# Second-layer weights of a routed MLP laid in SBUF by eight neighbouring rows for each partition

## The chip, the cores and the metric

The kernel runs on one core of one Trainium2 chip. The metric is the device time of one execution in microseconds (us), over several runs. Inputs lie in the chip's memory (DRAM) at the start, and the output must lie there at the end. The core's engines run side by side: TensorE multiplies matrices, VectorE, ScalarE and GpSimd do the element-wise work, and SyncE issues transfers. SBUF is the on-chip memory of 128 partitions; PSUM is the smaller one that TensorE writes its products to.

## The reference, cut to what matters

Two stages follow each other. The first is an attention of polynomial features, whose result becomes 4352 rows of 128 numbers. The second sends each row to two of eight experts, and each expert is a two-layer network:

```python
def _moe_ref(x, w_gate, w_noise, noise, w1, w2):      # x: 4352 x 128
    N, D = x.shape
    E = w_gate.shape[1]                                # 8 experts
    logits = x @ w_gate
    noise_scale = np.log1p(np.exp(x @ w_noise))
    noisy_logits = logits + noise_scale * noise
    top2 = np.argpartition(-noisy_logits, 2, axis=1)[:, :2]
    ...                                                # top2_w: softmax over the two
    for e in range(E):
        for k in range(2):
            mask = top2[:, k] == e
            h = np.maximum(x[mask] @ w1[e], 0.0)       # w1[e]: 128 x 1024
            out[mask] += top2_w[mask, k, None] * (h @ w2[e])   # w2[e]: 1024 x 128
```

Everything is float32. What matters here is the pair `h = max(x @ w1, 0)` and `h @ w2`: the second product sums over the 1024 hidden units, and a sum does not care in which order its terms come, as long as row f of `w2` meets hidden unit f.

## The kernel before, in words

**Layout of the weights.** Both weight tensors are kept in SBUF for the whole run. `w1s` has the 128 inputs of a row on the partitions and the 1024 hidden units of each expert beside each other. `w2s` is `[128 partitions, 8 experts, FJ = 8 pieces, D = 128]`; piece j of partition p holds row 128*j + p of the expert's `w2`. Function `load_w(e)` (line 377) issues the two transfers of an expert on SyncE's queue, through the helper `dma` (the transfer itself is recorded at line 338). `load_w` is called for expert 0, then 1, then 2 to 5, and last 6 and 7; between these calls stand the loads of the next keys, values and queries and of the padding of the row store `xs`.

**Blocks and waves.** After the router the rows of each expert are scattered by GpSimd into a store in DRAM, `xs`, at increasing places for each expert. Function `block` (line 1030) takes one stretch of one expert's rows. A wave is eight blocks, one for each expert, with the same stretch. There are six waves: two of 128 rows, three of 256 rows, and a last one of 128 rows. With 128 rows a block has n = 1 row tile, with 256 it has n = 2. So three waves have n = 1 and three have n = 2.

**Inside a block.** The block's rows stand transposed in `bT` (128 inputs by 128 or 256 rows). Then, in groups of js = 4/n pieces of 128 hidden units:
- `first` (line 1092; the product is line 1094) does js products into a PSUM tile `hp`. The stationary operand, loaded into the array, is a slice of 128 columns of `w1s`; the moving operand is `bT`, 128*n columns.
- `relu` (line 1098) takes `hp` to the SBUF tile `h`, mostly on ScalarE (line 1102).
- `second` (line 1105; the product is line 1109) does 4 products into the PSUM tile `acc`. The stationary operand is a slice of 128 columns of `h`, the moving operand a piece of `w2s` (128 columns).

With n = 1 a block has 2 groups of 4 first and 4 second products. With n = 2 it has 4 groups of 2 first products, which move 256 columns each, and 4 second ones. At the end `acc` is copied to `y`, and GpSimd scatters `y` to the tensor `pairs` in DRAM (`pool_scatter`, line 805).

**What sets the order.** All work is recorded as jobs with an engine, an estimated cost and a priority; class `Plan` (line 38) puts the jobs in one order by these estimates (its `order`, line 88), and each engine's instructions stand in that order. The costs are functions of tile sizes (`mm`, `vec`, `act`). GpSimd's scatters are tied by an extra dependency to the latest eviction recorded before them (`paces`).

**Other lines that the profile and the prediction name.** Line 606: the features of keys and queries. 669: the sums of features times values. 717: transposes of features on TensorE. 728: the numerators, with 98 moving columns. 747: a VectorE sum over the four heads of `lh`, read with the heads innermost. 975: a VectorE sum over the eight experts of `f2`, read in order. 809: GpSimd's scatters. 1417: products without use at the beginning, which keep TensorE busy. 322: copies by ScalarE or VectorE. A function `outside` (line 1258) runs only if an expert gets more rows than planned; it loads its weights by itself and the change does not touch it.

Of the kernel before, what the change touches and what calls it, by code (L numbers as in the profile page):

```python
# [37 lines left out]
class Plan:  # L38
# [17 lines left out]
    def new(self, tag):  # L56
        return Buf(tag)
# [117 lines left out]
def kernel(  # L175
# [15 lines left out]
    P = nc.NUM_PARTITIONS  # L191
# [5 lines left out]
    FJ = F // P  # L197
# [30 lines left out]
    V, A, G, T, Y = nc.vector, nc.scalar, nc.gpsimd, nc.tensor, nc.sync  # L228
# [4 lines left out]
    def add(engines, cost, emit, **kw):  # L233

        if hold and engines in ("DVE", "PE"):
            kw["after"] = tuple(kw.get("after", ())) + tuple(hold)
        elif hold and engines == EV:
            engines = "ACT"
        return plan.add(engines, cost, emit, **kw)
# [65 lines left out]
    def mm(n):  # L305
        return max(0.205, 0.016 + 0.00162 * n)
# [6 lines left out]
    def either(n):  # L313
        return {"ACT": act(n), "DVE": vec(n)}
# [17 lines left out]
    def dma(q, o, i, r, w, prio, size=0, issue=0.45, after=(), done=None, margin=0.0):  # L332

        eng = {"SP": Y, "ACT": A, "POOL": G}
        waits = hold_dma[0]

        def emit(e):
            ins = eng[e].dma_start(o(), i())  # L338
            if waits is not None:
                behind(ins, "rows %d" % waits)  # L340
            if done:
                done(ins)
        job = add(q, issue, emit, r=r, w=w, prio=prio, lat=LAND, after=after, size=size)
        if waits is not None:
            held.setdefault(waits, []).append(job)
        job.margin = margin
        return job
# [26 lines left out]
    w1s = const.tile([P, E, F], F32, name="w1s")  # L374
    w2s = const.tile([P, E, FJ, D], F32, name="w2s")

    def load_w(e, prio):
        dma("SP", lambda: w1s[:, e, :], lambda: moe_w1[e], (), [("w1", e)], prio, size=524e3, issue=0.5)
        dma("SP", lambda: w2s[:, e, :, :], lambda: moe_w2[e].rearrange("(j p) d -> p j d", p=P),
            (), [("w2", e)], prio, size=524e3, issue=0.5)  # L380

    words = const.tile([2 * R, 2 * DH], U32, name="words")
# [400 lines left out]
    def behind(ins, *keys):  # L783
        for key in keys:
            for name in writers.get(key, ()):
                tc.add_manual_dep(ins.ins, name, DATA, reason="rows written before")
# [243 lines left out]
    def block(u, w, e, r, n):  # L1030
# [57 lines left out]
        js = 4 // n  # L1088
        for g in range(FJ // js):
            hp, h = new("hp"), new("h")  # L1090

            def first(_, g=g, hp=hp):
                for i in range(js):
                    T.matmul(hp.t[:, P * n * i:P * n * (i + 1)], lhsT=w1s[:, e, P * (js * g + i):P * (js * g + i + 1)],  # L1094
                             rhs=bT.t[:, 0:P * n], start=True, stop=True)
            add("PE", js * mm(P * n), first, lat=0.15, r=[bT, ("w1", e)], w=[hp], prio=p0 + 10 * g)

            def relu(en, hp=hp, h=h):
                if en == "DVE":
                    paces.append(V.tensor_scalar_max(h.t[:], hp.t[:], 0.0))  # L1100
                else:
                    paces.append(A.activation(out=h.t[:], in_=hp.t[:], func=AF.Relu))  # L1102
            add(EV, either(512), relu, r=[hp], w=[h], prio=TOP + u)

            def second(_, g=g, h=h):
                for i in range(js):
                    for c in range(n):
                        j = js * g + i
                        T.matmul(acc.t[:, D * c:D * c + D], lhsT=h.t[:, P * (n * i + c):P * (n * i + c + 1)],  # L1109
                                 rhs=w2s[:, e, j, :], start=(j == 0 and c == 0), stop=(j == FJ - 1), skip_group_check=True)  # L1110
            add("PE", 4 * mm(D), second, lat=0.15, r=[h, ("w2", e)], w=[acc], prio=p0 + 10 * g + 15)
# [238 lines left out]
    rest_of_queries = keys_values(0, 0, head=True)  # L1350
    load_kq(1, "k", 40)
    load_w(0, 41)
    first_loads = len(plan.jobs)
    for r in (0, P):
        clear(r, 43)
    load_w(1, 44)
    for e in range(2, E - 2):
        load_w(e, 46 + e)
# [98 lines left out]
```

## Time and profile before

| | |
|---|---|
| median of 3 runs | 353.58 us (353.15 to 354.06) |
| the profiled execution, as timed | 354.19 us |
| its span, from the first to the last instruction | 352.4 us |
| mean granted clock of TensorE | 0.996 |
| transfers | 41.16 MB, mean 117 GB/s |
| first products (line 1094), matmul records | 768 in all: 384 of 128 moving columns, 384 of 256 |
| second products (line 1109), matmul records | 1152 of 128 moving columns |
| weight loads, lines 1094 and 1109 | mean 191 and 192 ns |

Durations of TensorE's matmuls include the time in its pipeline, so eight matmuls in a row take much less than eight times their mean. The time that each adds is read from a run of them in the chain of waits, as its length divided by its count. PE is TensorE's matmuls and PEld its weight loads, which overlap the matmuls. A group's line gives the tiles written and read, the shapes, the count, then busy time and mean, then the idle time just before and what ended it. In each float32 product one weight load and one matmul are recorded twice, so 384 first products stand as 768 records. Line numbers in the profile are those of the kernel file.

The stretches of the run, from the same profile (us of busy time, and the mean busy share of the transfer engines):

| stretch, us | TensorE | VectorE | ScalarE | GpSimd | DMA share | records of line 1094 |
|---|---|---|---|---|---|---|
| 0 to 28 | 25.55 | 21.60 | 9.91 | 19.22 | 0.97 | 5 |
| 28 to 75 | 45.56 | 35.94 | 19.61 | 37.26 | 0.70 | 109 |
| 75 to 185 | 106.10 | 65.18 | 40.48 | 85.26 | 0.39 | 240 |
| 185 to 312 | 127.00 | 15.76 | 49.75 | 79.91 | 0.30 | 290 |
| 312 to 344 | 31.66 | 7.05 | 12.58 | 11.49 | 0.36 | 128 |

A record that lies across a border is counted on both sides.

### The profile page before, as it was taken

How to read it: one execution, taken by the hardware profiler on the slowest of the kernel's cores; microseconds unless marked ns; L12 is line 12 of the kernel's file. 1: busy time of each engine (PE TensorE's matmuls, PEld its weight loads, DVE VectorE, ACT ScalarE, POOL GpSimd, SP SyncE). 2: the span in 40 equal slices, each digit the busy share in tenths (PEclk: the TensorE clock that was granted, in tenths of full speed). 3: DMA queues.
4: the chain of work that ended last, by engine and by line, in shares of the span. 5: the costliest groups of instructions: out<-in, count | busy, mean ns of one | idle time of the engine just before them, and what ended most of it. 6: DMA issues, size and time to landing. Idle time of an engine off the chain costs nothing.

```text
span 352.4 us, 7473 instructions
## 1 busy us (share of the span) xinstructions
PE 337.6 (96%) x2585; PEld 314.5 (89%) x2586; DVE 146.6 (42%) x550; ACT 132.3 (38%) x297; POOL 233.8 (66%) x386
## 2 busy tenths in 40 slices
PE   8999999898999999899999999999999999999992
PEld 3858999898899999789999999999999999999991
DVE  6889885684943675293766000102011000001401
ACT  2343541442442333341343433343334333434330
POOL 8857668882998876879866888887633543354510
PEclk9999999999999999999999999999999999999998
DMA  7999839654411244911432311355315311114521
GB/s 208 347 341 219 301 89 316 243 174 87 79 43 47 54 78 76 287 53 31 81 63 48 64 50 39 67 149 147 69 31 146 106 32 24 30 31 139 162 80 37
DMA packets 68297, 41.16 MB, mean 117 GB/s; under 512 B 49301, under 2 KB 60438, under 8 KB 68256
## 3 DMA queue, kind: packets, MB, share of 16 engines
q1 hardware_dynamic: 62784, 30.92, 34.6%
q0 software_dynamic: 4736, 9.19, 7.9%
q10 hardware_dynamic: 736, 0.54, 0.6%
q8 instruction: 21, 0.34, 0.4%
q14 instruction: 20, 0.16, 0.2%
HBM read 24.17 MB, written 16.65 MB: 116 GB/s over the span
## 4 chain that ended last, share of the span: by engine, by line
PE 88%; DVE 3%; SPq 2%; DMA 2%; issue 1%; ACT 1%; POOL 0%; DVEq 0%; POOLq 0%; ACTq 0%
PE hp L1094 34%; PE acc L1109 34%; PE bank L606 5%; PE bank L728 4%; PE bank L669 4%; PE bank L717 2%; SPq L338 2%; DMA kq<-in_k_dram 1%; PE hp L1417 1%; PE acc L669 1%; PE turn L1046 1%; PE bank L1241 1%; DVE xg L986 1%; DMA xb<-xs 1%; PE bank L690 0%
## 5 line engine op out<-in xcount | busy, mean ns | idle before, releaser
L1109 PEld LDWEIGHTS acc<-w2s,h 128*128 128x128 f32 x1152 | 146.3, 192 | 5.2 <-issue 0.2
L1109 PE MATMUL acc<-w2s,h 128*128 128x128 f32 x1152 | 150.7, 275 | 0.0
L1094 PE MATMUL hp<-bT,w1s 128*128 128x128 f32 (+1 forms) x768 | 148.5, 329 | 1.7 <-DVE row L965 1.0
L1102 ACT ACTIVATE h<-hp 128x512 f32<-128x512 f32 x143 | 85.4, 597 | 130.2 <-PE hp L1094 111.8
L1094 PEld LDWEIGHTS hp<-bT,w1s 128*128 128x128 f32 x768 | 111.6, 191 | 7.9 <-issue 1.5
L809 POOL DMA_INDIRECT pairs<-y,ix x62 | 61.1, 986 | 58.8 <-ACT y L322 48.8
L809 POOL DMA_INDIRECT xs<-xg,to x72 | 74.3, 1032 | 26.6 <-DVE xg L986 12.8
L1084 DVE STREAM_TRANSPOSE bT<-xb 128x256 f32<-128x256 f32 (+1 forms) x40 | 15.6, 389 | 119.1 <-PE hp L1094 92.6
L808 POOL MEMSET zb<- 128x400 bf16 (+1 forms) x142 | 63.2, 445 | 0.2
L322 ACT COPY y<-acc 128x128 f32<-128x128 f32 (+1 forms) x48 | 15.3, 319 | 23.1 <-PE acc L1109 18.5
L728 PE MATMUL bank<-kvw,pT 128*128 128x98 f32 x144 | 18.2, 274 | 0.1
L1165 DVE TENSOR_TENSOR o<-pr 128x512 f32<-128x512 f32 (+2 forms) x13 | 6.7, 519 | 27.7 <-DMA pr<-pairs 27.6
L728 PEld LDWEIGHTS bank<-kvw,pT 128*128 128x128 f32 x144 | 17.3, 192 | 0.6 <-DVE kvw L322 0.3
L322 ACT COPY pT<-bank 128x512 f32<-128x512 f32 (+1 forms) x17 | 9.2, 549 | 12.3 <-PE bank L717 6.1
L669 PE MATMUL bank<-phk,vaug 128*128 128x128 f32 (+1 forms) x108 | 13.1, 277 | 0.0
L669 PEld LDWEIGHTS bank<-phk,vaug 128*128 128x128 f32 (+1 forms) x108 | 12.6, 191 | 0.4
L628 DVE TENSOR_TENSOR phk<-ab 128x512 f32<-128x512 f32 (+1 forms) x20 | 12.2, 629 | 0.4
L322 ACT COPY lo<-bank 128x256 f32<-128x256 f32 (+3 forms) x20 | 6.2, 326 | 16.2 <-PE bank L606 8.4
L628 DVE TENSOR_TENSOR phq<-ab 128x512 f32<-128x512 f32 (+1 forms) x20 | 12.0, 632 | 0.3
L717 PE MATMUL bank<-ident,phq 128*128 128x128 f32 x72 | 10.8, 277 | 1.1 <-ACT kvw L322 1.1
L606 PE MATMUL bank<-sk,kT 128*128 128x128 f32 (+1 forms) x64 | 9.2, 286 | 2.5 <-DVE kT L590 1.6
L606 PEld LDWEIGHTS bank<-sk,kT 128*128 128x128 f32 (+1 forms) x64 | 7.5, 184 | 4.3 <-DVE kT L590 2.3
(178 smaller groups left out, 245.4 us busy)
## 6 DMA issues: line engine op xcount, KB each, us to landing
xs<-pad SPq DMA_DIRECT2D x9, 516.0 KB
w1s<-in_moe_w_dram SPq DMA_DIRECT2D x8, 512.0 KB
w2s<-in_moe_w_dram SPq DMA_DIRECT2D x8, 512.0 KB
pr<-pairs SPq DMA_DIRECT2D x7, 512.0 KB
xb<-xs SPq DMA_DIRECT2D x96, 32.0 KB
kq<-in_k_dram SPq DMA_DIRECT2D x4, 544.0 KB
kq<-in_q_dram SPq DMA_DIRECT2D x4, 544.0 KB
vld<-in_v_dram SPq DMA_DIRECT2D x14, 128.0 KB
```

Of the source, the lines that this page charges most:

```text
L322: paces.append(A.copy(o, i) if e == "ACT" else V.tensor_copy(o, i))
L606: T.matmul(ps.t[rows, 2 * W * i:2 * W * i + 2 * W], lhsT=lhsT, rhs=sk[:].rearrange("p c h x -> p (c h x)"), start=True, stop=True)
L628: V.tensor_tensor(out=jobs[i][2].t[rows, jobs[i][1]:jobs[m - 1][1] + 1, :, :].rearrange("p c h (i j) -> p (c h) i j", i=R), in0=factors(i, ...
L669: T.matmul(kvp.t[:, P * a:P * a + P], lhsT=va.t[0:K, t, hs, :].rearrange("p h d -> p (h d)"), rhs=pk.t[0:K, t, hs, :].rearrange("p h f -> ...
L717: T.transpose(ps.t[:, c0:c0 + P], pq.t[:, t + i, 2 * a:2 * a + 2, :].rearrange("p h f -> p (h f)"), ident[:])
L728: T.matmul(ps2.t[:, c0:c0 + 2 * YW], lhsT=pT.t[:, P * (2 * i + a):P * (2 * i + a) + P], rhs=kvw.t[:, a, :], start=True, stop=True)
L808: G.memset(zb[:, 0:FIRST_SPACER if kind == "first" else SPACER], 0.0)
L809: ins = G.indirect_dma_start(**kw)
L1084: add("DVE", vec(P * n), lambda _: V.transpose(bT.t[:, 0:P * n], flat()), r=[xb], w=[bT], prio=TOP + u)
L1094: T.matmul(hp.t[:, P * n * i:P * n * (i + 1)], lhsT=w1s[:, e, P * (js * g + i):P * (js * g + i + 1)], rhs=bT.t[:, 0:P * n], start=True, st ...
L1102: paces.append(A.activation(out=h.t[:], in_=hp.t[:], func=AF.Relu))
L1109: T.matmul(acc.t[:, D * c:D * c + D], lhsT=h.t[:, P * (n * i + c):P * (n * i + c + 1)], rhs=w2s[:, e, j, :], start=(j == 0 and c == 0), st ...
```

## The change

```diff
     def load_w(e, prio):
         dma("SP", lambda: w1s[:, e, :], lambda: moe_w1[e], (), [("w1", e)], prio, size=524e3, issue=0.5)
-        dma("SP", lambda: w2s[:, e, :, :], lambda: moe_w2[e].rearrange("(j p) d -> p j d", p=P),
+        dma("SP", lambda: w2s[:, e, :, :], lambda: moe_w2[e].rearrange("(p j) d -> p j d", j=FJ),
             (), [("w2", e)], prio, size=524e3, issue=0.5)
...
             def first(_, g=g, hp=hp):
                 for i in range(js):
-                    T.matmul(hp.t[:, P * n * i:P * n * (i + 1)], lhsT=w1s[:, e, P * (js * g + i):P * (js * g + i + 1)],
+                    T.matmul(hp.t[:, P * n * i:P * n * (i + 1)], lhsT=w1s[:, e, :].rearrange("d (p j) -> d j p", j=FJ)[:, js * g + i, :],
                              rhs=bT.t[:, 0:P * n], start=True, stop=True)
```

Piece j of partition p of `w2s` now holds row 8*p + j of the expert's `w2`, not row 128*j + p. A partition's eight rows are neighbours in DRAM, so that what was eight separate rows of 512 bytes for each partition is one stretch of 4 KB. To meet these rows, piece j of the first product must give the hidden units 8*p + j for p = 0 to 127. Its stationary operand is therefore every eighth column of `w1s`, from column j on: 128 float32 numbers with a step of 8 numbers (32 bytes) in each partition, where it was 128 neighbours. `w1s` itself lies as before. The second product's code is the same, and each sum has the same terms in another order. The number of instructions and their order on every engine are the same in both kernels; the costs that the plan is made from do not depend on the step.

## The prediction

> **What bounds the kernel now.** I read the page's busy times first, then the chain of waits, then the chain in two short stretches, then the groups of instructions with shapes kept apart, and last the waits of TensorE.
>
> ```profile
> PE 337.6 (96%) x2585; PEld 314.5 (89%) x2586; DVE 146.6 (42%) x550; ACT 132.3 (38%) x297; POOL 233.8 (66%) x386
> PE 88%; DVE 3%; SPq 2%; DMA 2%; issue 1%; ACT 1%; POOL 0%; DVEq 0%; POOLq 0%; ACTq 0%
> ```
>
> TensorE is 88% of the chain that ended last, and its weight loads (PEld) are nearly as busy as its matmuls. So a microsecond added to TensorE's stream is a microsecond on the end, unless TensorE was waiting there anyway. The chain in the last wave (one row tile for each block) and in a wave of two row tiles, then three groups:
>
> ```profile
> 312.73 0.89 PE hp L1094 x8
> 313.62 0.89 PE acc L1109 x8
> ...
> 263.54 0.87 PE hp L1094 x4
> 264.41 0.89 PE acc L1109 x8
> ...
> 36.35 1.76 PE bank L728 x16
> ...
> L1094 PE MATMUL hp<-bT,w1s 128*128 128x256 f32 x384 | 98.9, 380 | 0.7 <-ACT h L1102 0.7
> L1094 PE MATMUL hp<-bT,w1s 128*128 128x128 f32 x384 | 49.6, 277 | 1.0 <-DVE row L965 1.0
> L728 PE MATMUL bank<-kvw,pT 128*128 128x98 f32 x144 | 18.2, 274 | 0.1
> L1094 PEld LDWEIGHTS hp<-bT,w1s 128*128 128x128 f32 x768 | 111.6, 191 | 7.9 <-issue 1.5 <-ACT h L1102 1.1 <-ACT bT L322 0.2
> ```
>
> Eight matmul records take 0.89 us: one every 112 ns (0.89/8) with 128 rows moving, one every 217 ns (0.87/4) with 256. The program has 384 first products and the trace 768 records, because each float32 product is recorded as two pairs of load and matmul. The line to dwell on is L728: only 98 columns move, 23% fewer than 128, and still one record every 110 ns (1.76/16). If the moving side set the pace it would be 217*98/256 = 83 ns. What holds it at 110 is the load of 128 weight columns. So a load of 128 float32 columns lying side by side takes about 108 to 110 ns, and at 128 moving rows load and matmul are level: no slack above the load. At 256 moving rows there are about 107 ns of slack.
>
> TensorE's idle time ended by others is small; the largest are
>
> ```profile
> PE bank L606 <- DVE kT L590: 1.6, 2, 1.4
> PE hp L1417 <- DVE zb L439: 1.3, 1, 1.3
> PE bank L717 <- ACT kvw L322: 1.1, 1, 1.1
> ```
>
> and no load of w1s or w2s is among them.
>
> **What the Trainium skill says.** "SBUF — State Buffer", section on the two sides of SBUF (note on cachelines), and "Advanced Engine Details and Errata", section Memory Cachelines, say that SBUF works in lines of 16 bytes, that at least two hits on a line are needed to cover the latency of the memory, and that an access to a new line each time costs; they put no number on it. Contiguous float32 gives four hits to a line; every eighth float32 is 32 bytes on, one hit. "TensorE: Matmul & The Clock Gate", section LDWEIGHTS, prices a load at its columns divided by 1.2 GHz, 107 ns for 128; the 108 to 110 above agree. No strided stationary operand occurs in the trace, but VectorE reads one strided operand:
>
> ```profile
> L747 DVE TENSOR_REDUCE lg<-lh 128x32 f32<-128x128 f32 x16 | 5.9, 371 | 0.5
> L747 DVE TENSOR_REDUCE lg<-lh 128x16 f32<-128x64 f32 x4 | 1.0, 260 | 0.1
> L975 DVE TENSOR_REDUCE at<-f 128x18 f32<-128x144 f32 x3 | 0.9, 303 | 0.1
> ```
>
> L747 sums over the heads, so its inner step is 16 float32, 64 bytes. From 64 to 128 elements it goes from 260 to 371 ns: 1.73 ns an element. L975 reads contiguously: 144 elements in 303 ns and, by the line's own durations, 64 in 222: 1.01 ns. So a new line for each element costs 0.72 ns more, or reads at 1.73 ns a line; the trace agrees with the pages in kind. (L747 also has the shorter inner run, 4 against 8, so not all of it must be the step.)
>
> **The change, part by part.** No instruction is added, removed or reordered on any engine. *The w2 loads:* eight transfers of 512 KB, each 1024 pieces of 512 bytes before and 128 rows of 4 KB after, issued between 7.6 and 52.4 us on SP's queue. That can only shorten them and what queues behind them on SP (k and q of batch 1, v, the clears). TensorE waits for none of these by name; DMA share is 0.97 in the first 28 us and 0.70 up to 75 us, so a little of TensorE's early waiting may shrink. I bound it by 0 and 1 us and take 0.3. *Second products:* same loads, same moving rows of 128 contiguous columns: nothing. *First products:* 768 weight loads step 32 bytes. With rate 1.73 ns a line, 128 columns take 222 ns; with the contiguous load doubled, 2*108 = 216. I take a spacing of 218. Lower bound of a real penalty on top of today's load: 108 + 128*0.72 = 200, spacing 204; upper bound 230.
>
> Each spacing is the longer of the incoming load and the running matmul, since the next load runs beside the matmul:
> - 128 moving rows, 384 records: 112 becomes 218, +106 ns: 40.7 us. Nothing lies beside them; load and matmul are level today.
> - 256 moving rows, first load of each group: it runs beside the last second product of 128 columns, which covers only 112. Three waves, 8 experts, 4 groups: 96 times 106 ns: 10.2 us.
> - 256 moving rows, the other 288: the running matmul of 217 covers a load of 218: 0.3 us.
> - first load of second products after them: contiguous, covered as before: 0.
>
> Sum 51.2 us. Off it come 0.3 for w2 and about 0.9 for early waits that a later TensorE finds already over (its named waits above are 4 us together, mostly before 75 us or inside chains that move along with it): +50. ScalarE and VectorE (38% and 42% busy) wait longer on L1094; GpSimd's scatters are tied to the evictions and move along. The profiled execution took 354.19 us, 352.4 of it span; 354.2 + 50 = 404. It stood 0.6 above the median of the runs, less than the uncertainty here: I say 404.
>
> **The rivals.**
> 1. *The step is free for a weight load (not slower).* Place: the port that feeds the array. For: the float32 load may be paced by the array, not by the memory. The transposes at L717 load the same 128 float32 columns with records of 144 ns against 192 at L728, so the port can deliver 48 ns sooner than the products ask. If the strided read stays within 108 ns, nothing is lost and only the shorter w2 transfers remain. It decides from 108 ns a load downward. Against: a rate of 1.73 ns a line does not get 128 lines into 108 ns. Time: 353.6, between 352.6 and 354.2.
> 2. *The penalty is partly hidden.* If the 0.72 ns come on top of the port's faster time: 108 - 48 + 92 = 152, spacing 156: 384*0.044 + 96*0.044 = 21 us, 375. A like time comes if the work before 185 us, where GpSimd is 78% busy (37.3 of 47 us from 28 to 75 us, 85.3 of 110 after that), turns out to be bound by the scatters: 256 of the 384 records of 128 rows and a quarter of the group starts lie there, 27 + 3 us of the 51, and 21 would remain: 375. Against that, TensorE is busy for 45.6 of the 47 and 106.1 of the 110 us there, with hardly a named wait.
> 3. *The penalty is larger than the matmul of 256 rows.* Every line costs three times today's read: load 324; 384*0.212 + 96*0.212 + 288*0.107 = 133 us, 487. For: two passes read the same columns anew, and nothing in the trace caps the penalty on this port. Against: VectorE's 1.73.
>
> **How the numbers follow.** Forecast 0.65, rival one 0.19, rival two 0.11, rival three 0.05. The forecast's own range: spacing 204 gives 480*0.092 = 44, so 397; spacing 230 gives 480*0.118 + 288*0.013 = 60, so 414; a little around it for waits: 392 to 418. To hold 8 in 10 the range takes in rival two and the foot of rival three: 366 to 424. A measurement of this kernel tells 0.3%, about 1 us, from no change. Slower 0.81 (forecast and rivals two and three); rival one splits into faster 0.09, if w2's transfers are worth more than I give them, and same 0.10.
>
> **What would show it.** In the groups, the mean of L1094's weight loads rises from 191 to about 300 ns while L1109's stays at 192. In the chain of the last wave, eight hp records take about 1.75 us, not 0.89, and the acc records after them keep 0.89. In the waves of two tiles the four hp records and eight acc records take together 1.86 us, not 1.76: one late start a group. The last wave alone (128 records from 312 to 344 us) grows by 13.6 us. w2s packets become fewer and larger. I am wrong if hp keeps 0.89 for eight; wrong in size if 256-row records spread beyond 220 ns.

## The result and the profile after

| | before | after |
|---|---|---|
| median | 353.62 us | 415.12 us (414.82 to 415.16) |
| span of the profiled execution | 352.4 us | 413.4 us |
| transfer packets | 68297 | 61129 |

The changed kernel takes 1.1741 times as long (95% interval 1.1709 to 1.1774), 61.5 us more. The forecast was 404 us within 366 to 424: right in direction and mechanism, 11 us short in size. Ratios here and below are taken over the runs, not as quotients of the medians shown, and can differ from those by 0.1 to 0.2%.

The busy times and the chain by engine, from the page of the changed kernel:

```profile
PE 402.9 (97%) x2586; PEld 388.1 (94%) x2586; DVE 146.3 (35%) x550; ACT 132.3 (32%) x297; POOL 232.3 (56%) x386
PE 95%; DVE 2%; issue 0%; POOL 0%; ACT 0%; DVEq 0%; POOLq 0%
```

All the growth is TensorE's: the other engines have the busy time they had. The chain is now TensorE for 95%, and the shares of SyncE's queue and of transfers (2% each before) have gone from it. The groups of weight loads, shapes kept apart:

```profile
L1094 PEld LDWEIGHTS hp<-bT,w1s 128*128 128x128 f32 x768 | 193.0, 332 | 1.6 <-ACT h L1102 1.0 <-issue 0.3 <-ACT bT L322 0.2
L728 PEld LDWEIGHTS bank<-kvw,pT 128*128 128x128 f32 x144 | 17.3, 192 | 0.5 <-DVE kvw L322 0.3
```

The loads of L1094 went from a mean of 191 to 332 ns. L728, which loads the same shape from neighbouring columns, stayed at 192. The matmuls of L1094, shapes apart:

```profile
L1094 PE MATMUL hp<-bT,w1s 128*128 128x256 f32 x384 | 117.1, 428 | 0.7 <-ACT h L1102 0.7
L1094 PE MATMUL hp<-bT,w1s 128*128 128x128 f32 x384 | 97.8, 402 | 0.0
```

With 128 moving columns the busy time doubled (49.6 before), with 256 it rose by 18% (98.9 before): most of the price falls where the matmul is too short to cover its load. The chain of waits of the changed kernel, in the last wave and in a wave of two row tiles:

```profile
357.61 1.90 PE hp L1094 x8
359.50 0.89 PE acc L1109 x8
...
301.15 1.06 PE hp L1094 x4
302.21 0.89 PE acc L1109 x8
```

Eight records of first products take 1.90 us where they took 0.89: one every 238 ns, not 112. Four with 256 moving columns take 1.06, not 0.87. The second products between them keep 0.89.

These lines give the sum. Three waves of one row tile have 3*8*2 = 48 groups of eight records, each longer by 1.01 us: 48.5 us. Three waves of two row tiles have 96 groups of four, each longer by 0.19: 18.2 us. Together 66.7 us, and the span grew by 61.0. Most of the other 5.7 us comes off because TensorE now finds waits already over when it arrives. The waits listed for it add up to 8.0 us before and to 3.8 after. Four of them make that difference: L606 for `kT` (1.6, in the list ahead, and 0.3 now), L717 for `kvw` (1.1, now gone), and two that the list ahead leaves out, which are gone too. The two, and then L606 as it stands now:

```profile
PE hp L1094 <- DVE row L965: 1.0, 1, 1.0
PE bank L606 <- DVE lim L998: 0.8, 1, 0.8
...
PE bank L606 <- DVE kT L590: 0.3, 1, 0.3
```

So 4.2 of the 5.7 us are accounted for; the rest was not followed. The longest of the four shows what a chain of waits does and does not say. In the kernel before, the chain runs through the load of the keys just ahead of the features of batch 2; below it stands what TensorE did at that time:

```profile
142.49 5.04 DMA kq<-in_k_dram
...
147.56 0.72 DVE kT L590
148.28 0.04 issue
148.33 3.58 PE bank L606 x28
```

```profile
145.92 1.05 PE L1109 MATMUL acc<-w2s,h 128*128 128x128 f32 x8
148.33 1.94 PE L606 MATMUL bank<-sk,kT 128*128 128x128 f32 x15 [1.35 <-DVE kT L590]
```

The chain stands for 5.04 us in the transfer, but TensorE multiplied through most of that stretch and sat idle for 1.35 us only. In the changed kernel it comes to the same work straight from its own products:

```profile
176.75 0.89 PE acc L1109 x8
177.65 3.26 PE bank L606 x28
```

### The profile page after: what moved, and what is told of

Its sections match the earlier page's. It is cut to its first block, busy times and chain, and to the rows that moved or that the text cites. A ratio compares the mean times of both kernels' runs of the same rounds, so it can differ in the third digit from the quotient of the medians.

```text
span 413.4 us, 7474 instructions
## 1 busy us (share of the span) xinstructions
PE 402.9 (97%) x2586; PEld 388.1 (94%) x2586; DVE 146.3 (35%) x550; ACT 132.3 (32%) x297; POOL 232.3 (56%) x386
## 2 busy tenths in 40 slices
DMA packets 61129, 41.16 MB, mean 100 GB/s; under 512 B 49301, under 2 KB 52246, under 8 KB 61088
## 4 chain that ended last, share of the span: by engine, by line
PE 95%; DVE 2%; issue 0%; POOL 0%; ACT 0%; DVEq 0%; POOLq 0%
PE hp L1094 47%; PE acc L1109 31%; PE bank L606 4%; PE bank L728 4%; PE bank L669 3%; PE bank L717 2%; PE hp L1417 1%; PE acc L669 1%; PE turn L1046 1%; PE bank L1241 1%; PE bank L690 0%; DVE o L1040 0%; PE bank L937 0%; DVE lg L747 0%; ACT h L1102 0%
## 5 line engine op out<-in xcount | busy, mean ns | idle before, releaser
L1094 PE MATMUL hp<-bT,w1s 128*128 128x128 f32 (+1 forms) x768 | 214.9, 415 | 0.7 <-ACT h L1102 0.7
L1094 PEld LDWEIGHTS hp<-bT,w1s 128*128 128x128 f32 x768 | 193.0, 332 | 1.6 <-ACT h L1102 1.0
L1109 PEld LDWEIGHTS acc<-w2s,h 128*128 128x128 f32 x1152 | 148.5, 193 | 2.8 <-issue 0.2
L809 POOL DMA_INDIRECT xs<-xg,to x72 | 73.4, 1019 | 37.2 <-ACT h L1102 19.8
L728 PE MATMUL bank<-kvw,pT 128*128 128x98 f32 x144 | 18.2, 274 | 0.0
L728 PEld LDWEIGHTS bank<-kvw,pT 128*128 128x128 f32 x144 | 17.3, 192 | 0.5 <-DVE kvw L322 0.3
L1417 PE MATMUL hp<-zb 128*128 128x512 bf16 x30 | 9.6, 456 | 1.6 <-DVE zb L439 1.3
L986 DVE TENSOR_TENSOR xg<-x,g 128x512 f32<-128x512 f32 (+1 forms) x16 | 11.1, 747 | 0.0
L614 DVE TENSOR_TENSOR ab<-bank,lo 128x256 f32<-128x256 f32 (+3 forms) x20 | 7.2, 362 | 10.6 <-ACT lo L322 10.5
L717 PE MATMUL bank<-ident,phq 128*128 128x128 f32 x72 | 10.8, 276 | 0.0
```

Source lines behind the costliest of these rows:

```text
L717: T.transpose(ps.t[:, c0:c0 + P], pq.t[:, t + i, 2 * a:2 * a + 2, :].rearrange("p h f -> p (h f)"), ident[:])
L728: T.matmul(ps2.t[:, c0:c0 + 2 * YW], lhsT=pT.t[:, P * (2 * i + a):P * (2 * i + a) + P], rhs=kvw.t[:, a, :], start=True, stop=True)
L809: ins = G.indirect_dma_start(**kw)
```

## The experiments

Times are set beside runs of the kernel before on the same chip at the same time: 353.26 us for x1 to x4, 353.16 for x5 to x7, 354.78 for x8 and x9.

### The two parts of the change by themselves

x1, the w2 transfers alone:

```diff
-        dma("SP", lambda: w2s[:, e, :, :], lambda: moe_w2[e].rearrange("(j p) d -> p j d", p=P),
+        dma("SP", lambda: w2s[:, e, :, :], lambda: moe_w2[e].rearrange("(p j) d -> p j d", j=FJ),
```

> Only the w2 transfers are changed (eight neighbouring rows for each partition); w1 is read in order, so hidden units and rows of w2 do not match and the output is not the reference's. Theory A (the strided weight load is the whole cost): 353 us, between 352.5 and 354; w2 packets fewer and larger, first products at 112 ns a record. Theory B (part of the 61 us comes from the new transfers and what they collide with): above 357 us.

Measured: 352.74 us, ratio 0.9999 (0.9974 to 1.0024). Its page counts the packets:

```profile
DMA packets 61129, 41.16 MB, mean 117 GB/s; under 512 B 49301, under 2 KB 52246, under 8 KB 61088
```

The transfers did change: 7168 packets fewer than before, which is 896 (1024 less 128) for each of the eight transfers. It buys no time that can be measured, and costs none.

x2, the strided read alone:

```diff
-                    T.matmul(hp.t[:, P * n * i:P * n * (i + 1)], lhsT=w1s[:, e, P * (js * g + i):P * (js * g + i + 1)],
+                    T.matmul(hp.t[:, P * n * i:P * n * (i + 1)], lhsT=w1s[:, e, :].rearrange("d (p j) -> d j p", j=FJ)[:, js * g + i, :],
```

> Only the first products read every eighth column of w1; the w2 transfers are as before, so hidden units and rows of w2 do not match and the output is not the reference's. Theory A: 415 to 416 us, the whole growth, and 238 ns a record of the first products. Theory B: below 412 us, the rest being the transfers'.

Measured: 415.05 us, ratio 1.1748 (1.1709 to 1.1787), with the span of the changed kernel, 413.4 us. The strided weight load is the whole growth, to within the 1.4 us of the interval; theory B has fallen.

### What about the step costs: its lines, its size, or that there is one

x3 and x4 do the whole computation with two and with four neighbouring rows of w2 in a partition (n stands for 2 or 4):

```diff
-        dma("SP", lambda: w2s[:, e, :, :], lambda: moe_w2[e].rearrange("(j p) d -> p j d", p=P),
+        dma("SP", lambda: w2s[:, e, :, :].rearrange("p (a j) d -> p a j d", j=n), lambda: moe_w2[e].rearrange("(a p j) d -> p a j d", p=P, j=n),
...
-lhsT=w1s[:, e, P * (js * g + i):P * (js * g + i + 1)],
+lhsT=w1s[:, e, :].rearrange("d (a p j) -> d a j p", p=P, j=n)[:, (js * g + i) // n, (js * g + i) % n, :],
```

> The same computation as the changed kernel with two neighbouring rows of w2 for each partition in place of eight: w1 is read with a step of 2 (8 bytes), two hits on each 16-byte line, and w2 comes in pieces of 1 KB. Theory A1 (a line costs two float32 reads, so two hits hide it): 353 us, records of 112 ns. Theory A2 (any step other than 1 costs): about 415 us, records near 238 ns. Theory A3 (the cost grows with the step): in between, 368 us or so.

Measured: 354.60 us, ratio 1.0036 (1.0021 to 1.005): slower by 1.3 us, close to nothing, though the interval lies above 1. Theory A1 had the records at 112 ns; they stand at 118. The chain of waits of x3, in the last wave:

```profile
312.89 0.94 PE hp L1094 x8
```

> The same with four rows: w1 is read with a step of 4 (16 bytes), one hit on each line. Theory A1 (lines): the same as step 8, 414 to 416 us and 238 ns a record. Theory A2 (any step): the same. Theory A3 (grows with the step, or with the distance): clearly less, 370 to 400 us.

Measured: 411.34 us, ratio 1.1642 (1.1604 to 1.1681): nearly the whole price, at half the step, but 2.7 us under the lower end of what theory A1 gave. The chain of waits of x4, in the last wave:

```profile
373.73 1.86 PE hp L1094 x8
```

x5 and x6 read w1 with steps of 3 and 5, w2 as before (n stands for 3 or 5):

```diff
-lhsT=w1s[:, e, P * (js * g + i):P * (js * g + i + 1)],
+lhsT=w1s[:, e, 32 * (js * g + i):32 * (js * g + i) + n * P].rearrange("d (p j) -> d j p", j=n)[:, 0, :],
```

> First products read w1 with a step of 3 (12 bytes), from other columns than they should, so the output is not the reference's; w2 as before. Four elements lie on three lines. Theory A1 in the form of a rate (every line costs 1.7 ns, or two reads): 128*0.75*1.7 = 163 ns a load, some 170 to 185 ns a record, about 375 to 385 us. In the form of a threshold (free below 16 bytes, full price from there): 353 to 354 us and 112 ns a record.

Measured: 378.43 us, ratio 1.0701 (1.0635 to 1.0766). The chain of waits of x5, in a wave of two row tiles and in the last wave:

```profile
327.31 0.93 PE hp L1094 x4
...
361.14 1.39 PE hp L1094 x8
```

1.39 us for eight is 174 ns a record: the form of a rate, within its 170 to 185, and not the threshold.

> First products read w1 with a step of 5 (20 bytes), from other columns than they should, so the output is not the reference's; w2 as before. Theory A1 (one line for each element, whatever the distance): as step 8, 414 to 416 us and 238 ns a record. If the price came from a step that is a power of two (banks): clearly below, 354 to 390 us.

Measured: 403.52 us, ratio 1.1409 (1.1338 to 1.1479). Most of the price is there without a power of two, but the line "as step 8" missed: step 5 is the cheapest of the three that meet a new line each time. The chain of waits of x6, in the last wave:

```profile
364.06 1.78 PE hp L1094 x8
```

Side by side, each spacing being the time of eight first-product records in the last wave's chain, divided by eight. "Lines" are the 16-byte lines of the prediction on which 128 float32 lie at that step:

| step | bytes | lines | eight records | spacing | ns a line |
|---|---|---|---|---|---|
| 1 | 4 | 32 | 0.89 us | 112 ns | |
| 2 | 8 | 64 | 0.94 us | 118 ns | 1.84 |
| 3 | 12 | 96 | 1.39 us | 174 ns | 1.81 |
| 4 | 16 | 128 | 1.86 us | 233 ns | 1.82 |
| 5 | 20 | 128 | 1.78 us | 223 ns | 1.74 |
| 8 | 32 | 128 | 1.90 us | 238 ns | 1.86 |

One rule carries all six rows to within 8 ns: a spacing is the longer of 112 ns (the ordinary load) and about 1.8 ns for every line. Theory A2 (any step) falls with step 2, A3 (the size of the step) with step 4 against 8, and the threshold with step 3. Powers of two explain at most the 10 to 15 ns between step 5 and steps 4 and 8; what makes that difference was not tried.

### Which products pay

x7, the step of 8 in the waves of two row tiles alone:

```diff
-lhsT=w1s[:, e, P * (js * g + i):P * (js * g + i + 1)],
+lhsT=(w1s[:, e, :].rearrange("d (p j) -> d j p", j=FJ)[:, js * g + i, :] if n == 2 else w1s[:, e, P * (js * g + i):P * (js * g + i + 1)]),
```

> The step of 8 only in the three waves of two row tiles; the waves of one row tile read w1 in order; w2 as before, so the output is not the reference's. From the chain of the changed kernel: 1.06 in place of 0.87 us for each of 96 groups, 18 us: 371 to 372 us, less what early waits give back. By the working of the prediction (the load beside 256 moving rows hidden but for the first of each group, spacing 218): 10.5 us, 364 us.

Measured: 369.49 us, ratio 1.0471 (1.0392 to 1.0551), 16.3 us more (13.8 to 19.5). From the chain of waits of x7, a group of each kind:

```profile
325.20 1.06 PE hp L1094 x4
...
353.95 0.89 PE hp L1094 x8
```

The interval holds what the chain of the changed kernel said, 96*0.19 = 18.2 us less what waits give back, and leaves out the 10.5 us of the prediction's working.

### The last 20 ns, and the other operand

In the changed kernel a strided load after contiguous ones takes 217 ns until the next load starts, but 238 when it follows another strided one. The starts of four loads in a wave of two tiles show it, 0.21, 0.24 and 0.24 us apart:

```profile
302.83 0.31 PEld L1094 LDWEIGHTS hp<-bT,w1s 128*128 128x128 f32 x1
303.04 0.34 PEld L1094 LDWEIGHTS hp<-bT,w1s 128*128 128x128 f32 x1
303.28 0.34 PEld L1094 LDWEIGHTS hp<-bT,w1s 128*128 128x128 f32 x1
303.52 0.33 PEld L1094 LDWEIGHTS hp<-bT,w1s 128*128 128x128 f32 x1
```

x8 asks whether the moving operand beside it is to blame, by striding the second products' stationary operand, which has w2s beside it:

```diff
-                        T.matmul(acc.t[:, D * c:D * c + D], lhsT=h.t[:, P * (n * i + c):P * (n * i + c + 1)],
+                        T.matmul(acc.t[:, D * c:D * c + D], lhsT=h.t[:].rearrange("f (m k) -> f k m", k=4)[:, n * i + c, :],
```

> The second products take their stationary operand h with a step of 4 (every fourth column of a 512-column tile, so rows are mixed and the output is not the reference's); first products and w2 as before. If the price belongs to the stationary operand and 20 of the 233 ns a record come from one strided load following another: 233 ns a record, 1152*0.121 = 139 us more, about 490 us. If the 20 ns came from the moving operand bT that is read beside it: 214 to 217 ns a record, about 472 us.

Measured: 480.06 us, ratio 1.3523 (1.3335 to 1.371). The chain of waits of x8, in a wave of two tiles and in the last wave:

```profile
364.50 1.76 PE acc L1109 x8
...
460.83 1.86 PE acc L1109 x8
462.70 0.89 PE hp L1094 x8
```

1.86 us for eight, 233 ns: the same as step 4 in the first products, with another operand and another moving side. So bT is not the cause; that any moving operand read beside the load would do the same is not excluded. The time is 10 us below the expectation, and the chain shows most of why: in the waves of two tiles a group takes 1.76 us, not 1.86, since its first strided load runs beside a matmul of 256 columns. 96*0.10 = 9.6 us of the 139 are hidden in this way.

x9 strides the moving operand instead:

```diff
-                                 rhs=w2s[:, e, j, :], start=(j == 0 and c == 0), stop=(j == FJ - 1), skip_group_check=True)
+                                 rhs=w2s[:, e, :, :].rearrange("p j d -> p (j d)").rearrange("p (d j) -> p j d", j=FJ)[:, j, :], start=(j == 0 and c == 0), stop=(j == FJ - 1), skip_group_check=True)
```

> The second products stream w2 with a step of 8 (every eighth number, so the output is not the reference's); all stationary operands are read in order. If the line price holds for the moving side too: 217 ns or more a record in place of 112, 1152*0.105 = 121 us or more, from 474 us. If the moving side does not pay it: 353 to 354 us.

Measured: 488.38 us, ratio 1.3757 (1.3575 to 1.3939). The groups of x9, and its chain in the last wave:

```profile
L1109 PE MATMUL acc<-w2s,h 128*128 128x128 f32 x1152 | 290.2, 411 | 0.0
L1109 PEld LDWEIGHTS acc<-w2s,h 128*128 128x128 f32 x1152 | 232.5, 205 | 26.2 <-issue 0.2
```

```profile
469.91 1.86 PE acc L1109 x8
471.77 0.89 PE hp L1094 x8
```

Here the matmuls grew (411 ns, 275 before) and the loads hardly did (205 ns, 192 before), yet the spacing is again 233 ns. A step of 8 costs TensorE nearly the same on both of its operands, 233 and 238 ns a record. Only this one step was tried on the moving side, so that the price there goes by the line, as it does for the loads, is likely but not shown.

## Why the prediction was right, and where it fell short

- **What bounds.** Right. A microsecond on TensorE's stream was nearly a microsecond on the end: 66.7 us on the stream, 61.0 on the span. The reading of L728, that a load of 128 columns had no slack at 128 moving columns, is what the doubled busy time of that shape shows.
- **The price per line, taken from VectorE.** Right in kind, and close: 1.73 ns an element from L747, 1.74 to 1.86 ns a line on TensorE (the changed kernel and x3 to x6). Part of the closeness may be luck: L747 also had the shorter inner run, and no run varied a step on VectorE. The Trainium skill, "SBUF — State Buffer", section "SBUF: two separate sides" (note on cachelines), says that two hits on a line are needed for full bandwidth; steps of 3, 4, 5 and 8 agree. At step 2 the measurement adds a remnant, 118 ns where 112 was the contiguous spacing.
- **The spacing of 218 ns.** This is the term that was too small. A strided load behind a contiguous one does take 217 ns, as the doubling said. But behind another strided load the spacing is 238, and the sum used 218 for all 384 records of 128 columns: 384*0.020 = 7.7 us short. I had put 230 as the upper bound of the term. The 48 groups of these records begin with a load of 217, but the contiguous load behind each group takes 20 ns more, so the count of 384 stands.
- **The other 288 records of 256 columns.** "Covered, 0.3 us" failed for the same reason: 238 ns are not covered by a matmul of 217. With 21 ns for each of the 288 that is 6.0 us. The cover I counted on had no margin, and a load 10% longer than estimated showed through it: the sign of being wrong in size that I had named, records of 256 rows beyond 220 ns, came. x7 measured this part: 16.3 us where the working gave 10.5.
- **First load of each group.** 96 times 106 ns was right: the load that follows contiguous ones is the 217 ns one. The contiguous load after each group also starts some 20 ns late; in the chain above it is part of the 1.06 us, and 96 times that is the last 1.8 us by which the sum of 51.2 fell short of 66.7.
- **What comes off.** 1.2 us were forecast, about 5.7 came off. The way was right, a later TensorE finds waits over, but the 0.9 us for it had no working behind it. I took the named waits to lie mostly early or to move along; of the four that shrank, the longest was at 148 us, and two were not in my list. This error went the other way from those above: the sum on TensorE was 15.5 us short, the waits 4.5 us, and so the forecast was only 11 us off. That the two cancelled in part was luck.
- **The w2 transfers.** 0.3 us was taken; x1 shows 0 within 0.9 us either way, which does not tell 0.3 from nothing.
- **The rivals.** The free step falls with x2 and x4. The partly hidden penalty falls with the spacing of 238, and its second form, that the scatters bound the first 185 us, with the lines of the same work shown above: the features of L606 that began at 148.33 us begin at 177.65, 29 us later; had the scatters been the bound, most of that would have been absorbed. The penalty larger than 256 rows was nearer the truth than I gave it: the load does exceed the matmul of 256 columns, by 21 ns, but three times today's load is excluded.

No version here beats the kernel before: with the transfers worth nothing (x1), every step above 1 that was tried only adds to the loads, and x3 is the cheapest of them at 1.3 us.

## What to carry to other kernels

Before trading a longer piece in a transfer for a step in an operand, count the 16-byte lines that the operand touches: four neighbouring float32 share one line. Here every line cost TensorE about 1.8 ns on the stationary side wherever that came to more than the 112 ns of an ordinary load, so a step of four or more doubled the time of a load of 128 columns; a step of 8 on the moving side cost nearly as much. Ask too whether the transfer was on the path at all; here its new form alone changed nothing that could be measured (x1). And when one operation only just covers another, price the overrun: here a covered load 10% longer than estimated showed on every product of 256 columns.

## What the runs showed that I had not expected

The price follows the count of lines down to step 2: 64 lines, 118 ns, against 112 for the ordinary load: two hits on a line do not quite hide the step. The first strided load after contiguous ones takes 217 ns, each later one 238, and the contiguous load behind a strided group takes 131 where it took 112 (in the waves of one tile). So some 20 ns fall on whatever load comes behind a strided one, contiguous or not. A like pattern holds on the moving side in x9 (212 ns, then 233 in a row). Why this is so no run here shows. And step 5 is cheaper than steps 4 and 8 by 10 and 15 ns a load, though all three meet a new line with each element.
